# P times V of a gated attention and FFN kernel: its copy out of PSUM divided between VectorE and ScalarE

## The chip, the cores and the metric

The kernel runs on one core of a Trainium2 chip. The metric is the device time of one execution in microseconds, median of several runs.

## What is computed

Two branches share one input x of 2048 rows and 640 columns, and a gate per row mixes them:

```python
g = _sigmoid((x * gate_w).sum(-1, keepdims=True))
a = _A_ref(x, A_wq, A_wk, A_wv, A_wo, A_beta)
b = _B_ref(x, B_w1, B_w3, B_w2)
return g * a + (1 - g) * b
```

Branch B is a gated FFN (width 1728, SiLU). Branch A is an attention of 32 heads of 20 columns, in 4 segments of 512 rows: causal softmax inside a segment, plus a linear memory that carries sums of the earlier segments; both are mixed per head and go through `wo`. For each head and segment the part that matters here is

```python
logits = jnp.einsum("bhqd,bhkd->bhqk", qs, ks) * scale + mask
p = _softmax(logits, axis=-1)
a_dot = jnp.einsum("bhqk,bhkd->bhqd", p, vs)
```

## The kernel before

All matmul results land in PSUM, in eight banks of 128 partitions by 512 fp32 columns. `bank_tile` (line 111) hands the banks out in rotation: a tile gets the bank that was given out longest ago, and its first matmul must wait until the engine that read the former tile of that bank is done with it. Most projections run as three matmuls per block of 128 rows, on parts of the operands split in two, to reach fp32 accuracy.

The order on TensorE is the order in which the program issues matmuls; the other engines' instructions are put into an order by a scheduler at build time, and each engine then works through its own queue in that order. Two streams are interleaved on TensorE:

- Filler: the dense work (projections `proj`, line 249, for q, k, FFN gate `g` and up `u`; `v_blocks`, line 344; `ffn_down`, line 519, with tiles `f`; `oproj`, line 767), cut into steps by `yield`, each with a cost in ns.
- Attention: `attention` (line 740) goes through quads of four heads (32 quads in all). Per quad there are 40 slots; at slot 5 (`BIG`) and slot 17 (`SMALL`) it makes a visit, in which several pieces are issued together, with no filler between them. One loop in the main part spends the filler's costs against the slots.

The pieces of a visit (line 737) belong to different quads, as in a software pipeline:

- `s_fill` (line 573): scores q times k, 128 query rows by up to 512 keys, into two banks (`s`), one for each head of a pair. VectorE then takes the row maxima with a fused mask and maximum (line 588, tile `junk`), from which `max_rows` makes extra rows of q, to be subtracted inside the next product.
- `t_fill` (line 604): the same product transposed, keys by queries, again two banks (`t`). ScalarE takes exp out of the bank into the tile `P` (line 620), and POOL zeroes what lies over the diagonal (line 624).
- `pv_quad` (line 629): P times V of four heads, 16 matmuls, into one bank (`o`), 32 partitions to a head: 20 columns of V, one column of ones for the sum, and padding. VectorE copies the bank to the SBUF tile `oq` (line 638, one buffer) and SyncE's queue stores it to `od` in HBM (line 640), from where it is gathered later (`o_load`, line 674; `o_sums`, line 649) to be normalised and multiplied by `wo`.

The big visit issues, in this order: `s` fill 0 of the current quad; `t` fills 0 and 1 of the quad before; P times V of the quad two before; `t` fill 3, `s` fill 2, `t` fill 2, `s` fill 1. In the text these are called by their letter and number (`t3`, `s2`, `t2`, `s1`). `s1` is a pair of tiles of 384 and 128 columns, four matmuls in turn: first tile, second tile, first, second. Filler follows right behind.

SyncE's queue also carries the weight loads (`w_load`, line 154), loads of V (line 561) and the stores of projections (line 272). POOL's queue issues the loads of q and k (line 558), and POOL splits the weights (lines 174 and 175).

Of the kernel before, what the change touches and what calls it, by code (L numbers as in the profile page):

```python
# [38 lines left out]
def gated_mix(ctx: ExitStack, tc: tile.TileContext, xT, wqk, wv, w13, w2, w2h, wo, beta, out):  # L39
    nc = tc.nc  # L40
# [70 lines left out]
    def bank_tile(name, hold=None):  # L111


        k = free.pop(0)
        ps = pp.tile([P, L], F32, tag=f"b{k}", name=name, bufs=1)
        if hold:
            held[k] = -hold
        else:
            free.append(k)
        return ps  # L120
# [508 lines left out]
    def pv_quad(p):  # L629

        ps = bank_tile(f"o{p}")
        for kb, (o, n) in enumerate(PSEG):
            for i in range(4):
                nc.tensor.matmul(ps[32 * i:32 * i + 32, kb * P:], heads[2 * p + i]["v"][:, kb],  # L634
                                 pairs[p + i // 2]["P"][:, i % 2, o:o + n],
                                 start=kb == 0, stop=kb == 3, skip_group_check=True)
        ot = sp.tile([P, L], F32, tag="oq", name=f"oq{p}", bufs=1)
        nc.vector.tensor_copy(ot, ps)
        c, h = heads[2 * p]["c"], heads[2 * p]["h"]
        nc.sync.dma_start(od[c][h:h + 4].rearrange("h e n -> (h e) n"), ot)  # L640
        q = p // 2 % 8
        for b in OUT.get(q, ()):
            after(8, o_load, c, b)
        if q == 7:
            after(6 if c < NSEG - 1 else 2, o_sums, c)
# [77 lines left out]
    def after(n, f, *a):  # L723
        soon.append([n, f, a])
# [15 lines left out]
    def attention():  # L740

        for m in range(-1, NQUAD + 2):
            for n in range(40):
                if m == -1 and n < 40 - LEAD:
                    continue

                todo = VISITS.get(n, ()) if m != 1 else {BIG: VISITS[BIG][:3], BIG + 6: VISITS[BIG][4:]}.get(n, VISITS.get(n, ()))
                todo = [(kind, m - q, f) for kind, q, *f in todo if 0 <= m - q < NQUAD]
                if todo:
                    yield "amid" if len(todo) < 4 else "between"  # L750
                    for kind, q, f in todo:
                        if kind == "o":
                            pv_quad(2 * q)
                        else:
                            (s_fill if kind == "s" else t_fill)(q, *f)
                    if n == SMALL and 0 <= m < NQUAD:
                        after(4, max_rows, 2 * m)
                elif n in ((24, 36) if m < 0 else (BIG + 7, SMALL + 1)) and m + 1 < NQUAD:
                    load_pair(2 * (m + 1) + (n > BIG + 7 if m >= 0 else n > 24))
                tick()  # L760
                yield m
# [262 lines left out]
```

## Time and profile before

| | |
|---|---|
| median of 3 runs | 1109.91 us (1107.6 to 1111.63) |
| the profiled execution's own time | 1109.41 us |
| its span, first to last instruction | 1107.7 us |
| TensorE busy | 1094.4 us |
| VectorE busy | 592.6 us |
| ScalarE busy | 381.2 us |
| POOL busy | 584.7 us |

In the profile PE is TensorE's matmul part and PEld its weight loads; DVE is VectorE, ACT ScalarE, SP SyncE. A `q` behind an engine means its sequencer. A row names the source line, the engine, the operation, and the tiles as out<-in, with buffer numbers left out; a row of the timeline has the start, the time that the merged instructions span, their count, and in brackets the idle time before the first and what ended it. A row of the grouped view has the count, the busy time in us and the mean of one in ns, and then the idle time of the engine just before them. Ends of matmuls are modelled and matmuls overlap, so a PE that is busy by the profile may still have been held up; the starts tell more than the spans.

### The profile page before, as it was taken

The numbers are of one execution on the slowest core, as the hardware profiler recorded it, in microseconds if no ns is written. First come the engines' busy times: TensorE is split into PE (matmuls) and PEld (weight loads), VectorE is DVE, ScalarE is ACT, GpSimd is POOL, SyncE is SP. The second block draws the span as 40 slices with busy tenths as digits, with TensorE's granted clock in tenths as the row PEclk, the third lists the DMA queues.
The fourth block names the chain that finished last, engine by engine and source line by source line (L and its number), as shares of the span: only waits on it lengthen the run. The fifth ranks groups of instructions, "written<-read, shape, count | busy, mean of one in ns | idle before, by whom it ended". The sixth has DMA issues, their size and how long they took to land.

```text
span 1107.7 us, 17867 instructions
## 1 busy us (share of the span) xinstructions
PE 1094.4 (99%) x6285; PEld 852.9 (77%) x6285; DVE 592.6 (53%) x1708; ACT 381.2 (34%) x826; POOL 584.7 (53%) x729
## 2 busy tenths in 40 slices
PE   9999999999999999999999999999999999999997
PEld 6988877777777777788977777777777777777786
DVE  5032564356555554366154678875557765551645
ACT  6244233343233122145244543424343332233120
POOL 5055556366366363565175547555764556565253
PEclk9999999999999999999999999999999999999999
DMA  9266943334165132636268967455654433432122
GB/s 327 89 205 220 282 123 82 95 82 125 46 165 127 53 82 93 156 95 196 95 203 269 288 203 193 104 156 144 162 136 113 108 96 94 113 103 87 51 79 95
DMA packets 87545, 153.20 MB, mean 138 GB/s; under 512 B 11584, under 2 KB 25184, under 8 KB 87456
## 3 DMA queue, kind: packets, MB, share of 16 engines
q1 hardware_dynamic: 63040, 106.30, 30.4%
q0 software_dynamic: 20384, 38.68, 15.8%
q10 hardware_dynamic: 4032, 7.08, 1.8%
q8 instruction: 50, 0.82, 0.3%
q14 instruction: 39, 0.32, 0.1%
HBM read 96.56 MB, written 54.54 MB: 136 GB/s over the span
## 4 chain that ended last, share of the span: by engine, by line
PE 91%; DVE 4%; DMA 1%; ACT 1%; issue 1%; POOL 1%; SPq 0%; ACTq 0%; DVEq 0%; POOLq 0%
PE f L534 16%; PE g L253 16%; PE u L253 15%; PE v L364 6%; PE k L253 6%; PE op L784 6%; PE o L634 6%; PE q L253 6%; PE s L581 5%; PE t L614 4%; PE nd L331 1%; PE pm L428 1%; DVE junk L588 1%; PE pkt L413 1%; PE gt L713 1%
## 5 line engine op out<-in xcount | busy, mean ns | idle before, releaser
L588 DVE CUSTOM_DVE_ANT_0 junk<-s,mask 128x256 bf16<-128x256 f32 (+3 forms) x512 | 250.5, 489 | 106.3 <-PE s L581 74.1
L620 ACT ACTIVATE P<-t 128x512 f32<-128x512 f32 (+1 forms) x384 | 172.5, 536 | 192.1 <-PE t L614 154.8
L253 PE MATMUL g<-X,W 128*128 128x512 f32 x840 | 208.7, 398 | 0.0
L175 POOL TENSOR_TENSOR W<-wr,W 128x640 fp32r<-128x640 f32 (+1 forms) x126 | 200.3, 1596 | 2.3
L174 POOL CAST W<-wr 128x640 fp32r<-128x640 f32 (+1 forms) x126 | 91.0, 726 | 207.5 <-PE f L534 46.9
L534 PE MATMUL f<-ht,W 128*128 128x512 f32 x820 | 196.6, 397 | 0.3 <-POOL W L175 0.3
L253 PE MATMUL u<-X,W 128*128 128x512 f32 x780 | 196.7, 399 | 0.0
L624 POOL TENSOR_SCALAR_AFFINE_SELECT P<-P 128x256 f32<-128x256 f32 x192 | 94.6, 501 | 180.8 <-ACT P L620 180.6
L253 PEld LDWEIGHTS g<-X,W 128*128 128x128 f32 x840 | 155.9, 188 | 36.7 <-issue 0.4
L534 PEld LDWEIGHTS f<-ht,W 128*128 128x128 f32 x820 | 152.7, 188 | 37.0 <-POOL W L175 0.8
L253 PEld LDWEIGHTS u<-X,W 128*128 128x128 f32 x780 | 144.0, 188 | 34.5 <-ACT P L620 0.3
L107 POOL TENSOR_TENSOR ht<-ft,ht 128x512 fp32r<-128x512 f32 x52 | 67.1, 1291 | 91.3 <-ACT ht L106 90.8
L558 POOL DMA_DIRECT2D qk<-qkd x128 | 83.5, 654 | 0.3
L581 PE MATMUL s<-qk 60*128 60x256 f32 (+3 forms) x512 | 78.2, 345 | 2.2 <-DVE m L588 1.0
L253 PE MATMUL k<-X,W 128*128 128x512 f32 x300 | 77.0, 403 | 0.0
L634 PE MATMUL o<-P,vg 128*32 128x512 f32 (+3 forms) x1024 | 75.5, 435 | 1.4 <-DVE on L714 1.4
L253 PE MATMUL q<-X,W 128*128 128x512 f32 x300 | 74.0, 400 | 1.3 <-DVE X L107 0.7
L493 ACT ACTIVATE ft<-g 128x512 f32<-128x512 f32 x52 | 31.2, 599 | 125.7 <-PE g L253 114.7
L494 DVE SCALAR_TENSOR_TENSOR fu<-ft,g 128x512 f32<-128x512 f32 x52 | 35.7, 686 | 68.1 <-ACT ft L493 59.1
L364 PE MATMUL v<-W,X 128*128 128x320 f32 (+1 forms) x480 | 71.6, 311 | 0.3 <-ACT P L620 0.3
L364 PEld LDWEIGHTS v<-W,X 128*128 128x128 f32 x480 | 71.0, 189 | 0.8 <-ACT P L620 0.6
L106 ACT CAST ht<-ft 128x512 fp32r<-128x512 f32 x52 | 32.2, 619 | 111.9 <-DVE ft L500 111.8
(118 smaller groups left out, 1170.1 us busy)
## 6 DMA issues: line engine op xcount, KB each, us to landing
qk<-qkd POOLq DMA_DIRECT2D x128, 240.0 KB, 4.2
wr<-in_w_dram SPq DMA_DIRECT2D x80, 320.0 KB
qkd<-qs SPq DMA_DIRECT2D x20, 512.0 KB
qkd<-ks SPq DMA_DIRECT2D x20, 512.0 KB
od<-oq SPq DMA_DIRECT2D x32, 256.0 KB
wr<-in_wo_dram SPq DMA_DIRECT2D x20, 320.0 KB
vg<-vd SPq DMA_DIRECT2D x16, 336.0 KB
xr<-in_xT_dram SPq DMA_DIRECT2D x20, 256.0 KB
```

Of the source, the lines that this page charges most:

```text
L107: (lo or nc.gpsimd.tensor_sub)(dst[:, 1], src, dst[:, 0].bitcast(F32))
L174: nc.gpsimd.tensor_copy(w[:, 0, :n], raw[:, :n])
L175: nc.gpsimd.tensor_sub(w[:, 1, :n], raw[:, :n], w[:, 0, :n].bitcast(F32))
L253: nc.tensor.matmul(ps, w[:, a, kb * P:(kb + 1) * P], x[:, b, kb, :], start=n == 0, stop=n == 14)
L364: nc.tensor.matmul(ps[:, :n1 - n0], x[:, a, kb, lb * P:(lb + 1) * P], wvt[kb][:, b, n0:n1], start=n == 0, stop=n == 14)
L534: nc.tensor.matmul(ps, w, h, start=n == 0, stop=n == len(ms) - 1)
L558: here(nc.gpsimd.dma_start(t[64 * i:64 * i + RH], qkd[c][RH * (h + i):RH * (h + i + 1)]))
L581: nc.tensor.matmul(ps[i][:, o:o + w], q[:, qb * P:(qb + 1) * P], key[:, :w], start=n == 0, stop=n == len(todo) - 1, skip_group_check=True)
L588: nc.vector.tensor_tensor_reduce(out=junk[:, :w], in0=ps[i][:, o:o + w], in1=mask[:, L - w:], scale=1.0, scalar=-3.0e38, op0=ALU.add, op1= ...
L620: last["exp"] = nc.scalar.activation(pairs[2 * m + k]["P"][:, i, o:o + n], ps[i][:, b:b + n], AF.Exp, scale=SCALE)
L624: nc.gpsimd.affine_select(d, d, pattern=[[0, 2], [0, n], [1, P]], base=0, channel_multiplier=-1, compare_op=ALU.is_ge, fill=0.0)
L634: nc.tensor.matmul(ps[32 * i:32 * i + 32, kb * P:], heads[2 * p + i]["v"][:, kb], pairs[p + i // 2]["P"][:, i % 2, o:o + n], start=kb == 0 ...
```

## The change

The copy at line 638 is cut in two halves of 256 columns. VectorE copies the first, ScalarE the second. Everything else is the same text; the lines behind move by one.

```diff
         ot = sp.tile([P, L], F32, tag="oq", name=f"oq{p}", bufs=1)
-        nc.vector.tensor_copy(ot, ps)
+        nc.vector.tensor_copy(ot[:, :256], ps[:, :256])
+        nc.scalar.copy(ot[:, 256:], ps[:, 256:])
         c, h = heads[2 * p]["c"], heads[2 * p]["h"]
         nc.sync.dma_start(od[c][h:h + 4].rearrange("h e n -> (h e) n"), ot)
```

## The prediction

> **What bounds the kernel now.** First the page: the busy times and the chain of work that ended last. Then every wait of the matmul engine (VectorE and ScalarE wait on it all the time, but that costs nothing while TensorE never stops). Then one attention visit, instruction by instruction, because the changed line runs only there.
>
> ```profile
> span 1107.7 us, 17867 instructions
> PE 1094.4 (99%) x6285; PEld 852.9 (77%) x6285; DVE 592.6 (53%) x1708; ACT 381.2 (34%) x826; POOL 584.7 (53%) x729
> PE 91%; DVE 4%; DMA 1%; ACT 1%; issue 1%; POOL 1%; SPq 0%; ACTq 0%; DVEq 0%; POOLq 0%
> ```
>
> TensorE (PE) is busy 1094.4 of 1107.7 us and carries 91% of the chain: it is the bound, and it works strictly in the order of its queue. So a microsecond by which one of its matmuls is held up is a microsecond of the result, unless a later wait is shortened by it. The waits of PE show that there is almost nothing to shorten; these are the longest of eleven rows, a later one and the last:
>
> ```profile
> PE o L634 <- DVE on L714: 1.4, 1, 1.4
> PE warm L860 <- DVE zero L857: 1.3, 1, 1.3
> PE s L581 <- DVE m L588: 1.0, 1, 1.0
> PE s L581 <- DVE fu L494: 1.0, 1, 1.0
> ...
> PE f L534 <- POOL W L175: 0.3, 1, 0.3
> ...
> PE t L614 <- DVE pq L287: 0.2, 1, 0.2
> ```
>
> These (engine, line, what it waited for, us in total, times, longest), some 7 us together, are all that a profile with modelled matmul ends calls idle. Short stalls hide inside the modelled spans, so they have to be read from starts. Here is the first visit in which P times V runs: first PE, then VectorE, then ScalarE, then ScalarE again from a window that begins 1 us later and so leaves out the first exponential.
>
> ```profile
> 174.56 0.83 PE L634 MATMUL o<-P,vg 128*32 128x256 f32 x16
> 175.32 0.50 PE L614 MATMUL t<-qk 62*128 62x512 f32 x2
> 175.66 0.40 PE L581 MATMUL s<-qk 60*128 60x512 f32 x2
> 175.90 0.40 PE L614 MATMUL t<-qk 62*128 62x256 f32 x4
> 176.13 0.57 PE L581 MATMUL s<-qk 60*128 60x384 f32 x4
> 176.63 1.66 PE L253 MATMUL u<-X,W 128*128 128x512 f32 x6
> ...
> 175.46 0.69 DVE L638 COPY oq<-o 128x512 f32<-128x512 f32 x1 [0.89 <-PE o L634]
> 176.09 0.69 DVE L588 CUSTOM_DVE_ANT_0 junk<-s,mask 128x512 bf16<-128x512 f32 x1
> ...
> 175.92 2.19 ACT L620 ACTIVATE P<-t 128x512 f32<-128x512 f32 x6 [0.96 <-PE t L614]
> ...
> 176.41 1.70 ACT L620 ACTIVATE P<-t 128x512 f32<-128x512 f32 x5
> ```
>
> After P times V (`o`) PE issues the pair `t3` (175.32), the pair `s2`, `t2`, then the pair `s1` (176.13) and then the woven-in projection (176.63). A visit takes 15 banks and there are eight in rotation, so a bank returns after seven others: the second tile of `s1` gets the bank of `o`. The copy of `o` ends at 175.46 + 0.69 = 176.15, just as `s1` begins. To see whether that end really holds PE, I take the visit in which VectorE came to the copy latest:
>
> ```profile
> 705.24 0.68 DVE L638 COPY oq<-o 128x512 f32<-128x512 f32 x1
> ...
> 705.78 0.68 PE L581 MATMUL s<-qk 60*128 60x384 f32 x4
> 706.40 1.66 PE L253 MATMUL g<-X,W 128*128 128x512 f32 x6
> ```
>
> Here the copy ends 0.14 us after the first `s1` matmul starts (705.92 against 705.78), 0.12 later than in the visit above (0.02). The projection follows 0.62 us after that start instead of 0.50: 0.12 later too. So the release of this one bank already sets PE's pace, one for one. That is the place of the change.
>
> **The change part by part.** Lines behind 638 move by one; I keep the old numbers, and call the new ScalarE line 639.
>
> *VectorE.* 32 copies of 512 columns become 32 of 256. The nearest rows are maxima of PSUM tiles, which cost the same as the copy at 512 columns:
>
> ```profile
> L638 DVE COPY oq<-o 128x512 f32<-128x512 f32 x32 | 22.1, 691 | 32.2 <-PE o L634 32.2
> L588 DVE CUSTOM_DVE_ANT_0 junk<-s,mask 128x512 bf16<-128x512 f32 x128 | 88.2, 689 | 50.6 <-PE s L581 43.3
> L588 DVE CUSTOM_DVE_ANT_0 junk<-s,mask 128x256 bf16<-128x256 f32 x128 | 54.3, 424 | 38.1 <-PE s L581 30.9
> ```
>
> Half a copy is therefore about 0.43 us and VectorE gains 0.26 x 32 = 8.4 us of its own time. It is busy 53%, so this is worth nothing by itself; its half ends at 175.46 + 0.43 = 175.89.
>
> *ScalarE.* 32 copies of 128x256 out of PSUM are added. The trace has no such copy, only wider and narrower ones:
>
> ```profile
> L372 ACT COPY V<-v 128x320 f32<-128x320 f32 x24 | 10.3, 427 | 36.5 <-PE v L364 36.5
> L432 ACT COPY mt<-pm 128x147 f32<-128x147 f32 x12 | 3.4, 285 | 17.6 <-PE pm L428 15.6 <-POOL W L175 2.0
> L620 ACT ACTIVATE P<-t 128x512 f32<-128x512 f32 x256 | 137.1, 600 | 192.1 <-PE t L614 154.8 <-DVE acc L542 18.8 <-DVE acc L795 9.0
> ```
>
> Between 285 ns at 147 columns and 427 at 320, 256 columns interpolate to 285 + 142 x 109/173 = 374 ns; 0.285 and 0.427 are the bounds. I take 0.37. The Trainium skill, page "ScalarE: Activation LUTs", section "What ACT_TABLE_LOAD costs", gives 186 ns + 0.833 ns per column for an instruction with immediate operands, so by its figures an estimate of 399 ns, with which the sum below would be 0.025 x 30 = 0.8 us more, 1128. The trace agrees within 6%: the 320-column row has 427 where that formula gives 453.
>
> *Where the copy stands.* What decides is the queue. In the compiled order ScalarE's copy stands behind the exponential of the first `t3` tile and ahead of the second, in 29 of the 30 visits that matter here; it waits for VectorE (and for the old store of `oq`, long landed). The second tile of `s1`, which waited for VectorE, now waits for ScalarE. VectorE's half is done at 175.89; the exponential ahead starts at 175.92, and the next ScalarE instruction started 0.49 later (176.41). So VectorE is not what ScalarE waits for: it is busy with the exponential. The copy begins at 176.41, ends at 176.41 + 0.37 = 176.78, and the bank is free 176.78 - 176.15 = 0.63 us later than before. Bounds: with the 147-column duration 0.54; with the 320-column one, no overlap with the exponential (which then ends first, 0.60 - 0.49 = 0.11 more) and 0.07 for a signal passed on (from the end of the last `o` matmul, 175.39, to the start of the copy, 175.46), 0.63 + 0.06 + 0.11 + 0.07 = 0.87.
>
> *Queued behind the copy.* The second `t3` exponential and the four of `t2` come later on ScalarE by the copy's share, at most 0.37 us. PE needs those banks only from the second projection tile on (the first holds 15 matmuls; six are 1.66 us), so this is hidden. The one exception is the visit whose woven-in tile is a short one:
>
> ```profile
> 515.92 0.57 PE L581 MATMUL s<-qk 60*128 60x384 f32 x4
> 516.84 1.00 PE L364 MATMUL v<-W,X 128*128 128x320 f32 x5 [0.35 <-ACT P L620]
> ```
>
> There PE already waits 0.35 for an exponential after `s1`, and of the 0.63 only about 0.63 - 0.35 = 0.28 remain.
>
> *The store and SyncE.* The store of `oq` now waits for ScalarE: 0.6 us later, and the weight loads behind it on SyncE's queue with it. In a few places the order on that queue moves by one (a load of V, one of weights or a gather of `od` ahead of or behind the store), and POOL swaps two steps of its weight splits once. No wait of PE on a DMA is in its list, so I cost these at nothing; their cover is the weight ring, loaded several tiles ahead, and if it failed it would show as PE waiting for POOL's split, 0.3 us in all today.
>
> *Sum.* 32 quads; the last two visits issue no `s1` any more, so 30 are hit. 30 x 0.63 = 18.9. Off: 0.35 in the visit above, 0.12 in the late one (its bank was already 0.12 later), 0.4 in the one visit where the compiled order puts the copy ahead of the `t3` exponential (the copy then runs from 175.96 to 176.33 in this clock, the exponential starts 0.3 late, ends at 176.82, and holds the projection by some 0.24). Together 0.9: **+18.0 us**. The profiled execution took 1109.41 us (span 1107.7 and 1.7 around it), 0.5 under the median 1109.91. 1109.4 + 18.0 = 1127.4, rounded to **1127 us** (1.6% slower).
>
> **The rivals.**
>
> *Taken back.* PE is late in each visit, but would have waited later anyway. For it: the bank of `s1` is already a wait today. Against it: the listed waits of PE are those 7 us in all, most of them ahead of the attention or single, so even if all were swallowed 11 us stay, 1120; for 1109 every visit would need 0.6 us of slack behind it, and the copy that came 0.12 late passed all of 0.12 on.
>
> *VectorE was the pace (ends faster).* If PE truly follows VectorE in the visit, 0.26 us less there in each visit is up to 0.26 x 32 = 8.4 us: 1101. It decides once ScalarE's half ends before the whole copy did, 0.69 after the start, so once it starts by 0.32 after; its place in the queue gives it 0.95 after (176.41 - 175.46). It would need ScalarE to have the copy ahead of the exponential.
>
> *The pause costs more than the copy.* If the copy must wait out the exponential, and PE, having stood still, resumes more slowly, 0.9 to 1.3 us a visit: 1109.4 + 27 to 39 - 0.9 = 1135 to 1147. For it: a pause of 0.6 us in the middle of `s1` is longer than any in these visits. Against: in the late visit PE stood still too, and lost no more than the delay.
>
> *It only costs the hand-over.* The change says "two halves", but ScalarE's waits for VectorE's. Were ScalarE idle there, the bank would be free after 0.43 + 0.07 + 0.37 against 0.69, so 0.18 x 30 = 5.4 us more: 1115. The exponential in front speaks against it in 29 of 30 visits.
>
> The Trainium skill, page "PSUM — Partial Sum Buffer", section "PSUM bank collisions raise a hardware error", says that two engines may not touch one bank in the same 32 partitions at once, even in disjoint columns. By that rule the halves can only follow one another, and this rival, not a gain, is the best that the split could give; were they free to overlap, an idle ScalarE would leave the time about as it is. No run here shows two engines reading one bank together; the compiled wait has the rule's form.
>
> **How the numbers follow.** The forecast, bank held by ScalarE's place in the queue: 0.74. Its own range by the bounds is 1109.4 + 30 x 0.54 - 0.9 = 1125 to 1109.4 + 30 x 0.87 - 0.9 = 1135. Taken back in part (1112 to 1121): 0.07; wholly (1109): 0.04; costs more (over 1135): 0.08; hand-over only (about 1115): 0.04; VectorE the pace (1101): 0.03. The range 1119 to 1136 takes in both ends of the forecast and the upper part of what may be taken back, and leaves out some 2 in 10. About 0.3% (3.3 us) is what a measurement of this kernel tells from no change: faster 0.03, the same 0.04, slower 0.93.
>
> **What the new profile would show.** Right: two groups of 32 copies, about 430 ns on VectorE and 370 on ScalarE; in a visit ScalarE's copy starting some 0.49 us after the `t3` exponential; the four `s1` matmuls stretched from 0.57 to about 1.2 us, and the projection 1.1 us after the first of them instead of 0.50; PE's sums by line unchanged but for L581, and nothing new in the waits of PE on POOL or DMA. Wrong: an `s1` group that stays near 0.57 us (then the bank was not the pace), ScalarE's copy ahead of the exponential, a copy that waits for VectorE, or a span that grows by another amount than 30 times the stretch of `s1`.

## The result, and the profile after

| | median, us | runs | ratio to before, 95% interval |
|---|---|---|---|
| before | 1108.76 | 4 (1107.53 to 1111.63) | |
| the change | 1126.43 | 4 (1124.84 to 1128.06) | 1.0145, 1.0129 to 1.0161 |

The change makes the kernel slower: by 17.7 us between the two medians, which are of four runs each, and by 14.3 to 17.9 us by the interval of the ratio (the ratio itself, 1.0145, is 16.1 us). 1127 us was forecast. The profiled execution took 1128.06 us, with a span of 1126.3.

First the page of the changed kernel: the span, the busy times and the chain by engine.

```profile
span 1126.3 us, 17913 instructions
PE 1102.6 (98%) x6285; PEld 855.4 (76%) x6285; DVE 586.2 (52%) x1708; ACT 390.0 (35%) x858; POOL 583.0 (52%) x729
...
PE 91%; DMA 3%; ACT 2%; issue 2%; DVE 1%; POOL 1%; SPq 0%; ACTq 0%; DVEq 0%; POOLq 0%
```

PE has the same 6285 matmuls and is still the bound, but it now stands still more. The waits of PE say where; these are the first rows and three of those that follow (engine, line, what it waited for, us in total, times, longest):

```profile
PE s L581 <- ACT oq L639: 10.7, 29, 0.7
PE o L634 <- DVE on L715: 1.4, 1, 1.4
...
PE q L253 <- ACT X L106: 0.9, 1, 0.9
PE s L581 <- DMA qk<-qkd: 0.7, 2, 0.5
...
PE t L614 <- DMA qk<-mr: 0.6, 1, 0.6
```

A wait that was not in the list before heads it: `s1` waits for ScalarE's half of `oq`, 29 times. Its 10.7 us are less than the time lost, because matmul ends are modelled and the first part of each stop hides in the span of the matmul ahead. The whole of it is in the starts. Here is the first visit of the changed kernel, PE, then VectorE, then ScalarE, to be laid beside the same visit in the prediction:

```profile
177.95 0.50 PE L614 MATMUL t<-qk 62*128 62x512 f32 x2
178.29 0.39 PE L581 MATMUL s<-qk 60*128 60x512 f32 x2
178.53 0.40 PE L614 MATMUL t<-qk 62*128 62x256 f32 x4
178.77 0.33 PE L581 MATMUL s<-qk 60*128 60x384 f32 x1
179.46 0.50 PE L581 MATMUL s<-qk 60*128 60x384 f32 x3 [0.37 <-ACT oq L639]
179.89 1.65 PE L253 MATMUL u<-X,W 128*128 128x512 f32 x6
...
178.09 0.42 DVE L638 COPY oq<-o 128x256 f32<-128x256 f32 x1 [0.89 <-PE o L634]
...
178.55 0.60 ACT L620 ACTIVATE P<-t 128x512 f32<-128x512 f32 x1 [0.96 <-PE t L614]
179.04 0.37 ACT L639 COPY oq<-o 128x256 f32<-128x256 f32 x1
179.29 1.72 ACT L620 ACTIVATE P<-t 128x512 f32<-128x512 f32 x5
```

VectorE's half is over at 178.51. Next in ScalarE's queue is the `t3` exponential, which starts at 178.55; ScalarE's half starts 0.49 us after that (179.04) and ends at 179.41. The second `s1` tile follows at 179.46. From the first `s1` matmul to the filler it is 179.89 - 178.77 = 1.12 us, 0.50 before.

Added up over the 30 visits, from the end of `o` to the filler, the changed kernel loses 17.8 us. The span differs by 18.6; the windows of the two profiles show the rest. A row has the window, its length, PE busy with its count, and so on, then the granted clock, the DMA share and GB/s; first the kernel before (its first 25 us; from the first `o` to the last; the tail), then the changed one:

```profile
0.00:25.00 25.00, 22.50 (x92) 15.71 (x93) 15.17 (x21) 16.57 (x27) 13.91 (x25) 1.00 0.92 334
...
173.03:1023.25 850.22, 846.12 (x5008) 648.61 (x5005) 482.03 (x1477) 305.08 (x669) 469.94 (x587) 1.00 0.48 132
1023.25:1107.70 84.45, 78.78 (x372) 61.91 (x371) 43.40 (x66) 9.67 (x16) 31.57 (x25) 1.00 0.23 74
```

```profile
0.00:25.00 25.00, 21.77 (x75) 14.69 (x76) 13.64 (x19) 14.99 (x25) 11.28 (x23) 0.93 0.83 304
...
175.66:1041.89 866.23, 852.40 (x5008) 649.35 (x5005) 476.38 (x1477) 313.57 (x700) 468.95 (x587) 1.00 0.47 129
1041.89:1126.30 84.41, 78.78 (x372) 61.97 (x371) 43.00 (x66) 10.03 (x17) 31.58 (x25) 0.98 0.23 74
```

Between the first and the last `o` the changed kernel needs 866.23 - 850.22 = 16.0 us more: the 17.8 of the visits, less 1.8 between visits. The tail is equal. The other 175.66 - 173.03 = 2.6 us arise before any changed line runs: in the first 25 us of this execution the loads came at 304 instead of 334 GB/s, PE got through 75 matmuls instead of 92, and the granted clock was 0.93. Profiles of the variants below have their first `o` between 172.5 and 173.6, among them two with the same split. So it belongs to this execution and not to the change. The 17.8 us of the visits and the 16.0 us net of them both lie inside the interval of the measured times (14.3 to 17.9), which doesn't tell them apart.

### The profile page after: what moved, and what is told of

Same layout as the page of the kernel before. It is cut to its first block, busy times and chain, and to the rows that moved or that the text cites. A ratio compares the mean times of both kernels' runs of the same rounds, so it can differ in the third digit from the quotient of the medians.

```text
span 1126.3 us, 17913 instructions
## 1 busy us (share of the span) xinstructions
PE 1102.6 (98%) x6285; PEld 855.4 (76%) x6285; DVE 586.2 (52%) x1708; ACT 390.0 (35%) x858; POOL 583.0 (52%) x729
## 4 chain that ended last, share of the span: by engine, by line
PE 91%; DMA 3%; ACT 2%; issue 2%; DVE 1%; POOL 1%; SPq 0%; ACTq 0%; DVEq 0%; POOLq 0%
PE g L253 17%; PE f L534 16%; PE u L253 16%; PE v L364 6%; PE o L634 6%; PE op L785 6%; PE k L253 6%; PE q L253 5%; PE s L581 4%; PE t L614 3%; PE nd L331 2%; PE pm L428 1%; ACT oq L639 1%; DMA oall<-od 1%; ACT P L620 1%
## 5 line engine op out<-in xcount | busy, mean ns | idle before, releaser
L620 ACT ACTIVATE P<-t 128x512 f32<-128x512 f32 (+1 forms) x384 | 176.2, 544 | 194.2 <-PE t L614 156.8
L581 PE MATMUL s<-qk 60*128 60x256 f32 (+3 forms) x512 | 85.3, 351 | 12.3 <-ACT oq L639 10.7
L581 PEld LDWEIGHTS s<-qk 60*128 60x128 f32 x512 | 46.6, 185 | 43.4 <-issue 20.7
```

The source lines that it names most:

```text
L581: nc.tensor.matmul(ps[i][:, o:o + w], q[:, qb * P:(qb + 1) * P], key[:, :w], start=n == 0, stop=n == len(todo) - 1, skip_group_check=True)
L620: last["exp"] = nc.scalar.activation(pairs[2 * m + k]["P"][:, i, o:o + n], ps[i][:, b:b + n], AF.Exp, scale=SCALE)
```

## The experiments

**Theory A**, that of the prediction: PE stops until the last copy out of the bank of `o` is done, and what stands ahead of that copy in its engine's queue decides when this is. The rivals tried here: **B**, ScalarE's added work is what costs; **C**, the serial hand-over from one engine to the other costs; **D**, the later store of `oq` and the moved order of SyncE's queue. Every kernel was timed beside runs of the kernel before on the same chip. Times "in the visits" are added up from the starts, as above.

### The whole copy on ScalarE

```diff
-        nc.vector.tensor_copy(ot, ps)
+        nc.scalar.copy(ot, ps)
```

> ScalarE makes the whole copy of 512 columns. In the compiled order it now stands ahead of the exponential of the first t3 tile. Theory A (the bank of o comes back when the last copy ends, and what stands ahead of that copy in ScalarE's queue sets this end): the copy starts some 0.07 us after the last matmul of o, takes 0.59, the second s1 tile starts as early as before, the filler at most 0.05 us per visit off: within 2 us of before, 1107 to 1111. Rival B (ScalarE's added time is what costs, 17.7 us per 256 columns): 1144. Rival C (only the hand-over between two engines costs): no hand-over, 1109; so A and C agree here, and B is told apart.

Measured: 1109.85 against 1109.82 us, ratio 0.9999 (0.9989 to 1.001). PE, then ScalarE, in the first visit:

```profile
175.83 0.47 PE L581 MATMUL s<-qk 60*128 60x384 f32 x4
176.29 1.65 PE L253 MATMUL u<-X,W 128*128 128x512 f32 x6
...
175.16 0.59 ACT L638 COPY oq<-o 128x512 f32<-128x512 f32 x1 [0.50 <-PE o L634]
175.64 2.20 ACT L620 ACTIVATE P<-t 128x512 f32<-128x512 f32 x6
```

Twice the columns on ScalarE, and nothing is lost: the copy runs in a gap of ScalarE's, ahead of the exponential, and ends at 175.75, before `s1` begins. `s1` to filler is 0.46 us. B, by which this should have taken 1144 us, is out.

### Only 32 columns on ScalarE

```diff
-        nc.vector.tensor_copy(ot, ps)
+        nc.vector.tensor_copy(ot[:, :480], ps[:, :480])
+        nc.scalar.copy(ot[:, 480:], ps[:, 480:])
```

> VectorE copies 480 columns, ScalarE only 32. In the compiled order the short copy stands behind both t3 exponentials. Theory A: it starts 1.50 us after the last matmul of o, takes some 0.19, so the second s1 tile starts at 1.74 instead of 0.81: 0.93 x 29 = 27 us more than before, 1136, and slower than with 256 columns. Rival B (ScalarE's time): an eighth of 17.7, 1111. Rival C (hand-over): 0.66 + 0.07 + 0.19 - 0.69 = 0.23 per visit, 7 us, 1116.

Measured: 1135.37 against 1109.82, ratio 1.023 (1.0213 to 1.0247), so 25.6 us; in the visits 27.5, and 0.93 in an ordinary one. PE, then ScalarE:

```profile
176.06 0.33 PE L581 MATMUL s<-qk 60*128 60x384 f32 x1
177.06 0.50 PE L581 MATMUL s<-qk 60*128 60x384 f32 x3 [0.67 <-ACT oq L639]
177.48 0.74 PE L253 MATMUL u<-X,W 128*128 128x512 f32 x2
...
175.84 1.08 ACT L620 ACTIVATE P<-t 128x512 f32<-128x512 f32 x2 [0.96 <-PE t L614]
176.81 0.19 ACT L639 COPY oq<-o 128x32 f32<-128x32 f32 x1
176.88 1.25 ACT L620 ACTIVATE P<-t 128x256 f32<-128x256 f32 x4
```

An eighth of the change's columns costs more than the change. The copy itself takes 0.19 us, but it stands behind two exponentials instead of one. VectorE's part was over at 176.04, so the hand-over (C) explains a small part at most.

### ScalarE's half first

```diff
-        nc.vector.tensor_copy(ot, ps)
+        nc.scalar.copy(ot[:, 256:], ps[:, 256:])
+        nc.vector.tensor_copy(ot[:, :256], ps[:, :256])
```

> Both halves as in the change, but ScalarE's is written first, and VectorE's waits for it. In the compiled order ScalarE's half stands ahead of the t3 exponential. Theory A: ScalarE's half from 0.07 to 0.45 after the last matmul of o, VectorE's from 0.52 to 0.94, the second s1 tile at 0.99 instead of 0.81: 0.18 x 30 = 5 us more than before, 1114. Rival B (ScalarE's time): as the change, 1126. Rival C (hand-over alone): 5 us, 1114, like A.

Measured: 1113.08 against 1109.82, ratio 1.0029 (1.0017 to 1.0042); in the visits 3.8. In the first visit the halves run, ScalarE first and then VectorE:

```profile
175.11 0.37 ACT L638 COPY oq<-o 128x256 f32<-128x256 f32 x1 [0.50 <-PE o L634]
...
175.52 0.42 DVE L639 COPY oq<-o 128x256 f32<-128x256 f32 x1 [1.30 <-ACT oq L638]
```

This is what the hand-over alone costs: 175.94 for the end of both, 0.83 us after the start, where one VectorE copy takes 0.69. The two are one behind the other here too.

### The change, with its copy ahead of the exponential

```diff
         for i in range(2):
             for k, o, b, n in outs:
                 last["exp"] = nc.scalar.activation(...)
+                if (f, i) == (3, 0):
+                    here(last["exp"])
...
-        nc.vector.tensor_copy(ot, ps)
+        nc.vector.tensor_copy(ot[:, :256], ps[:, :256])
+        nc.scalar.copy(ot[:, 256:], ps[:, 256:])
```

`here` orders an instruction behind the one written before it on its engine, which is ScalarE's half.

> The change itself, with one more ordering: the t3 exponential of the first tile is held behind ScalarE's half. Nothing else differs from the change in any instruction's shape. Theory A: every visit becomes like the one at 969 us in the profile of the change, where the copy ran from 0.53 to 0.90 and the filler came 0.21 later than before: 0.21 x 30 = 6 us, 1115. Rival B (ScalarE's time): still 1126. Rival C (hand-over): 0.18 x 30 = 5 us, 1114, but then the change itself should have been 1114 too.

Measured: 1114.69 against 1109.82, ratio 1.0047 (1.0032 to 1.0062). In the visits 6.0, in ordinary ones 0.21 as forecast. PE, ScalarE and VectorE:

```profile
176.15 0.70 PE L581 MATMUL s<-qk 60*128 60x384 f32 x4
176.86 1.42 PE L253 MATMUL u<-X,W 128*128 128x512 f32 x5
...
175.94 0.37 ACT L641 COPY oq<-o 128x256 f32<-128x256 f32 x1 [0.96 <-DVE oq L640]
176.21 2.20 ACT L620 ACTIVATE P<-t 128x512 f32<-128x512 f32 x6
...
175.48 0.42 DVE L640 COPY oq<-o 128x256 f32<-128x256 f32 x1 [0.89 <-PE o L636]
```

The same instructions as the change, in another order on one queue, give back 12 of its 18 us. Now ScalarE's half does wait for VectorE (175.48 to 175.90, then 175.94), and what remains is the hand-over and the pushed-back exponential.

### Another bank for `s1`, without and with the change

```diff
         ps = bank_tile(f"o{p}")
+        kept.append(free.pop())
...
                             (s_fill if kind == "s" else t_fill)(q, *f)
+                    if kept:
+                        free.insert(0, kept.pop())
```

(with `kept = []` beside `bank`.) The bank of `o` is set aside until the visit's other tiles have theirs, and then goes to the filler.

> The kernel before, with one change in the handing out of banks: the bank of o is set aside until s1 has its tiles and then goes to the filler, so the second s1 tile gets the bank of the first t3 tile. Theory A (PE goes on when the reader of the bank that it needs next is done): that exponential ends 1.12 us after the last matmul of o, the second s1 tile starts at 1.17 instead of 0.81, the filler at 1.60 instead of 1.24: 0.36 x 30 = 11 us, less little in two visits: 1119 to 1121. Any rival in which the bank of o does not matter: 1110.

> The change (both halves, ScalarE's behind the t3 exponential), with the same handing out of banks. Theory A: the second s1 tile waits for the exponential (1.12) and not for the copy (1.39), the filler's bank is free at 1.44, ahead of 1.60, so the split costs nothing any more: as bank_before, 1119 to 1121, and some 6 us less than the change. Rivals B (ScalarE's time) and D (the later store, the moved order of the DMA queue): bank_before plus 17.7, some 1137.

Measured: without the split 1119.48 against 1109.16, ratio 1.0094 (1.0075 to 1.0112); with it 1120.18, ratio 1.0097 (1.0082 to 1.0112). PE of the first visit, without and with:

```profile
176.45 0.93 PE L581 MATMUL s<-qk 60*128 60x384 f32 x4
177.31 1.42 PE L253 MATMUL u<-X,W 128*128 128x512 f32 x5
```

```profile
176.73 0.93 PE L581 MATMUL s<-qk 60*128 60x384 f32 x4
177.60 1.42 PE L253 MATMUL u<-X,W 128*128 128x512 f32 x5
```

With `s1` on the bank of a `t3` tile, both wait for the same exponential, 0.86 and 0.87 us from `s1` to filler, though ScalarE's half is still in its place in the queue. ScalarE in the first visit of the second kernel:

```profile
176.52 0.60 ACT L620 ACTIVATE P<-t 128x512 f32<-128x512 f32 x1 [0.96 <-PE t L614]
177.01 0.37 ACT L641 COPY oq<-o 128x256 f32<-128x256 f32 x1
```

In 27 of the 30 visits the split changes nothing; in the other three the filler comes 0.27 to 0.30 us later, 0.8 us together. In the last visit but one, which has no `s1` and is not one of the 30, the filler comes 0.6 us later, held by ScalarE's half, as this row of PE's waits shows:

```profile
PE g L253 <- ACT oq L641: 0.8, 1, 0.8
```

These four come to 1.5 us in the traces, and the medians are 0.7 us apart, with intervals that overlap, where the change itself cost 17.7. ScalarE's added work, the later store and the moved order of the other queue are all still there, so they cost no more than this by themselves (B and D are out); the 17.7 us need PE to want this bank next.

### Two halves, both on VectorE

```diff
-        nc.vector.tensor_copy(ot, ps)
+        nc.vector.tensor_copy(ot[:, :256], ps[:, :256])
+        nc.vector.tensor_copy(ot[:, 256:], ps[:, 256:])
```

> VectorE makes both halves of 256 columns, ScalarE none. Theory A: the second half starts some 0.06 us ahead of the end of the first, so the last copy ends at 0.85 instead of 0.76 after the last matmul of o, the filler 0.09 later: 0.09 x 30 = 3 us, 1112.5. A theory in which two copies in place of one cost as such: as the change, 1127.

Measured: 1112.85 against 1109.16, ratio 1.0029 (1.0017 to 1.0042); in the visits 3.3. The second half started 0.34 us after the first and the pair lasted 0.75 us, so the filler came 0.12 later rather than 0.09. Cutting the copy has a small price of its own, about as large as the hand-over; it is too small to be that of the change.

### ScalarE busy at the same place, on nothing

```diff
                 last["exp"] = nc.scalar.activation(...)
+                if (f, i) == (3, 0):
+                    side = sp.tile([P, P], BF, tag="side", name="side", bufs=1)
+                    for x in range(2):
+                        here(nc.scalar.copy(side, mask[:, x * P:(x + 1) * P]))
```

> The kernel before, with two added copies of 128 columns per quad on ScalarE, out of an SBUF constant into a tile that nobody reads; the first stands between the two t3 exponentials, where the change has its copy, the second a place or more behind. VectorE still makes the whole copy of o. Theory A: ScalarE's added time falls on nobody's bank until the filler's second tile: within 2 us of before, 1109 to 1111. Rival B (ScalarE's time): about the 17.7 us of the change, 1127.

Measured: 1110.08 against 1109.16, ratio 1.0012 (1.0 to 1.0024); 0.1 us in the visits. PE, then ScalarE, in the first visit:

```profile
176.67 0.57 PE L581 MATMUL s<-qk 60*128 60x384 f32 x4
177.17 1.67 PE L253 MATMUL u<-X,W 128*128 128x512 f32 x6
...
176.46 0.60 ACT L620 ACTIVATE P<-t 128x512 f32<-128x512 f32 x1 [0.96 <-PE t L614]
176.95 0.29 ACT L625 COPY side<-mask 128x128 bf16<-128x128 bf16 x1
177.14 0.60 ACT L620 ACTIVATE P<-t 128x512 f32<-128x512 f32 x1
```

The first of the two copies stands between the two `t3` exponentials, where the change has its own, and takes 0.29 us; the second `t3` exponential comes 0.68 after the first instead of 0.49. `s1` to filler stays at 0.50 us. A second time, ScalarE's added work costs nothing in the visits, and by the interval at most 2.7 us in all.

### An attempt at a faster visit

In the kernel before, the filler starts 0.07 us later than the `s1` matmuls alone would need (1.24 after the end of `o`, against 0.74 for the first `s1` matmul and 0.43 from the second tile to the filler). With the whole copy on ScalarE I issued `s2` ahead of `t3`:

```diff
-("o", 2), ("t", 1, 3), ("s", 0, 2), ("t", 1, 2), ("s", 0, 1))
+("o", 2), ("s", 0, 2), ("t", 1, 3), ("t", 1, 2), ("s", 0, 1))
```

> ScalarE makes the whole copy, ahead of the t3 exponential, and s2 is issued ahead of t3. In scalar_all the visit was 0.04 us shorter than before and the filler waited for the first t3 exponential (1.15). Theory A: the filler now gets the bank of the first s2 tile, whose maxima end near 1.0 on a VectorE without the copy, so the filler starts at the end of the s1 matmuls, 1.17 instead of 1.24: 0.07 x 30 = 2 us less than before, 0.9975 to 0.999. If the four t3 and t2 exponentials, now 0.3 us later, hold something else, equal or slower.

Measured: 1110.03 against 1109.45, ratio 1.0008 (0.9998 to 1.0017): no gain. The filler came at 1.22; its bank now belongs to an `s2` tile, whose maximum ended at 1.16, not at 1.0, and in the visit whose filler is a short tile 0.39 us were lost to a VectorE wait. The wait was exchanged for another of the same length. No version tried beats the kernel before.

## Why the prediction was right

- **The bound and the place.** PE in order, with the bank of `o` setting its pace, one for one: the late copy at 705 us was the evidence, and the two runs with another bank for `s1` are the proof.
- **The place in the queue.** The decisive step was to find ScalarE's half behind the `t3` exponential, not behind VectorE. Forecast 0.63 us for an ordinary visit, measured 0.62. The three visits taken off: 0.28 left in the one with the short tile (forecast 0.28), 0.51 in the late one (0.63 - 0.12), 0.21 in the one whose copy stands ahead (0.24). Five more visits leave the 0.62, which the prediction didn't foresee: three lose 0.56 or 0.57 and two 0.69 and 0.71. That these cancel is luck.
- **The durations.** Over the 32 copies ScalarE's half took 0.365 to 0.373 us, 0.367 in the middle (0.37 taken), VectorE's 0.424 (0.43). The estimate of 0.399 us by the Trainium skill, page "ScalarE: Activation LUTs", section "What ACT_TABLE_LOAD costs", is 9% above the measured one; the page gives its figure for an ACTIVATE, and the trace calls this instruction a COPY.
- **The sum.** +18.0 forecast, +17.8 in the visits, +17.7 between the medians. The 17.8 is what the prediction added up, and it is right. That the total fits as closely is partly luck: net of the stretches between visits it is 16.0, and 16.1 by the ratio.
- **"Taken back."** In this profile the stretches between visits are 1.8 us shorter together. That does not show that lost time was taken back: with ScalarE busy on nothing, which lost 0.1 us in the visits, they are 1.2 us shorter too, and with 32 columns on ScalarE, which lost 27.5, only 0.4. How much of the 1.8 belongs to the change stays open; the rival as a whole (1109) is out, and 1112 to 1121 with it.
- **Queues costed at nothing.** Nearly so: the list of PE's waits has two rows on DMA that were to be absent (0.7 and 0.6 us). The same two waits, 1.2 and 0.6 us, stand in the list of the kernel with two halves on VectorE, where ScalarE has no half to be late with. The first stands where the kernel before waits 1.0 us for VectorE, in its list too, and so is no added time. What brings these waits about was not tried.
- **The hand-over rival** was the right size for its case: 3.8 us with ScalarE first, 6.0 with the copy ahead of the exponential, 5.4 forecast for an idle ScalarE. It is part of the change's cost only where the exponential is out of the way.
- **The pause that costs more than the copy.** No row stood behind its price of 0.9 to 1.3 us a visit. PE resumes as fast as before: from the start of the second `s1` tile to the filler it is 0.43 us in the kernel before (0.81 to 1.24 after the end of `o`), 0.43 in the change (179.46 to 179.89) and 0.42 after the longer stop with 32 columns (177.06 to 177.48).
- **VectorE as the pace.** The 8.4 us of this rival were too much. With the whole copy on ScalarE the bank is free 0.11 us earlier than before (0.65 after the end of `o`, not 0.76), and the filler comes only 0.04 earlier: its own bank is that of the first `t3` tile, which the exponential reads until 1.15.

## What to carry to other kernels

What counted here, when a tile was read out of PSUM, was when its bank was free again, and whether the next matmul in order wanted that bank. ScalarE had spare time and did not help, because the instruction that it was given stood in its queue behind something longer: 32 columns behind two exponentials cost 26 us, 256 behind one 18, and 512 ahead of them nothing. So read the compiled order of the engine that is to take the work over before counting its free time, and look at the starts of the matmuls, not only at the listed waits, which showed 10.7 of 17.8 us.

## What was not expected

- A copy of 128x512 from PSUM took 0.586 us on ScalarE and 0.69 on VectorE, and with the whole copy on ScalarE VectorE was busy for 573.1 instead of 592.6 us without any change in the time that could be told from noise.
- In the profiled execution of the change the first 25 us ran at a granted clock of 0.93 and with slower loads, and the first `o` came 2.6 us later than before.
